# A three-part chain on one core: where the second MoE makes the next span's operand sums

## The chip, the cores and the metric

The kernel runs on one core of a Trainium2 chip. Its time is the device time in microseconds (us) of one execution; the median of three runs is compared. The engines of the core work side by side, each through its own list of instructions in order: TensorE (matmul), VectorE (called DVE in the rows), ScalarE (ACT), GpSimd (POOL) and SyncE (SP, which issues the DMAs here).

## What is computed

Decayed linear attention ("retention"), and two feed-forward stages on its 4608 tokens of width 512:

```python
x = retention(q, k, v)                          # 8 x 8 heads, 576 positions, width 64
h = max(x @ w1, x @ w2, x @ w3); x = h @ w_out  # first MoE, d_ff 768
h = x @ w_in                                    # second MoE: 512 -> 2048
g = h * clip(h + 3.0, 0.0, 6.0) / 6.0
out = g @ w_out                                 # 2048 -> 512
```

All of it is in float32 precision. The kernel gets that from split operands: a number is held as a high part (rounded by ScalarE to the type that TensorE takes) and a remainder (the difference, by VectorE), and a product is three matmuls: high x high, high x remainder, remainder x high.

## The kernel before

The change touches only how the second MoE makes the token operands of its first matmuls. That stage works on six *spans* of 768 tokens (index p), and in each span on eight *pairs* of hidden blocks (index j): a pair is 256 hidden units. In a pair the 512 x 768 tokens and the 512 x 256 weights are each cut in two by two, and the four hidden blocks C11, C22, C21 and C12 (128 x 384 each) come out of seven products instead of eight. Each product is six matmuls of 128x384. The products take, in this order, the token operands B11, B21, T2, T1, T3, T4, B22 (products 0 to 6), where the T's are sums of token quarters:

- T1 = B12 - B11, T2 = B22 - T1, T3 = B22 - B12, T4 = B21 - T2. Each is one subtraction on VectorE over 128x768 numbers (line 597), made in place in the span's tile `xf`: T1 takes B11's room, T3 takes B12's, T4 takes B21's.
- Each of the seven operands is then split (`split`, lines 53 to 56): ScalarE writes the high part (line 55, a CAST), and the remainder (line 56, VectorE) is put on a list, `late`. `flush()` empties that list into VectorE's order; it is called ahead of each projection job and ahead of each gate.

The function `operand(p, v, name)` does this for one operand. The operands of span p + 1 are made while span p is worked on: its tokens are loaded in pair 1, B11 and B21 are made in pair 4, T2 and T1 in pair 5, T3 and T4 in pair 7, and B22 in pair 0 of span p + 1 itself. B11, B21, T1 and T2 have a second set of tiles; T3, T4 and B22 have one, so their split may be written only when the last pair has read the old one (products 4, 5 and 6 of pair 7).

Two PSUM tiles, X and Y, hold the products of a pair, and the next pair uses the same two banks. What frees them is this. Product 0 goes to X, ScalarE copies it out (`kept`, line 674), products 2, 4 and 5 are added to X, with a copy after 2 and after 4; products 1, 3 and 6 go to Y. `added` (line 669, tile `cc`) adds Y and a copy, `gated` (lines 661 and 662, tile `g`) applies the activation and splits the result to tile `v`. C11 is gated after product 1, C22 after product 4, C21 after product 5 straight out of X, and C12 after product 6. So the next pair's product 0 waits for C21's line 662, and its product 1 for C12's line 669.

Between the products stand the projections: `project(2)` takes two jobs off a list of the pair before, each three matmuls of 128x512 (lines 703 to 705) that multiply a gated block by `w_out`. In pair 0 the last jobs of the span before are among them, and their results are brought out by ScalarE and VectorE in turn (`store`, lines 687 and 689).

The order of each engine's list is the order in which the code calls these functions (the schedule is manual); nothing reorders it later. The first span's operands are made in a loop beside the last tile of the first MoE, in the order `FRONT + BACK` (line 578).

Of the kernel before, what the change touches and what calls it, by code (L numbers as in the profile page):

```python
# [24 lines left out]
F1, F2 = FF1 // P, FF2 // P  # L25
# [4 lines left out]
NS = NT // TS  # L30
# [9 lines left out]
def retention_moe_moe2(ctx: ExitStack, tc, hi, lo, w_a, w_b, mask, qdec, kdec, grow, out):  # L40
# [3 lines left out]
    def f32(ap):  # L44
        return ap.bitcast(F32)
# [3 lines left out]
    def flush():  # L49
        while late:  # L50
            late.pop(0)()

    def split(full, hi, lo, eng=None):

        nc.scalar.copy(hi, full)  # L55
        late.append(lambda: (eng or nc.vector).tensor_tensor(out=lo, in0=full, in1=f32(hi), op=ALU.subtract))  # L56
# [16 lines left out]
    def x_tile():  # L73
        return x_pool.tile([P, 2, KM, TB], F32R, tag="x", name="x")
# [65 lines left out]
    def v_tile():  # L140
        return w_pool.tile([P, 2, 512], F32R, tag="v", bufs=NA - F2, name="v")
# [292 lines left out]
    def product(ps, w, cols, terms, first, last, read=False):  # L434

        xh, xl = terms
        wh, wl = w[:, 0, cols], w[:, 1, cols]
        nc.tensor.matmul(ps, lhsT=wh, rhs=xh, start=first, stop=False, skip_group_check=read)  # L438
        nc.tensor.matmul(ps, lhsT=wh, rhs=xl, start=False, stop=False, skip_group_check=read)  # L439
        nc.tensor.matmul(ps, lhsT=wl, rhs=xh, start=False, stop=last, skip_group_check=read)  # L440
# [45 lines left out]
    with tc.manual_schedule():  # L486
# [94 lines left out]
        def load_x2(p, room):  # L581

            full = room[:, :KM * TS].rearrange("p (k n) -> p k n", n=TS)
            n0 = 0
            while n0 < TS:
                t, c0 = divmod(p * TS + n0, TB)
                n = min(TB - c0, TS - n0)
                nc.sync.dma_start(out=full[:, :, n0:n0 + n], in_=x2_d[t][:, :, c0:c0 + n])
                n0 += n
            k2 = KM // 2  # L590
            return {"B11": full[:, :k2, :TH], "B12": full[:, :k2, TH:], "B21": full[:, k2:, :TH],
                    "B22": full[:, k2:, TH:], "X": room[:, KM * TS:].rearrange("p (k n) -> p k n", n=TH)}

        def operand(p, v, name):

            def put(out, a, b):
                nc.vector.tensor_tensor(out=out, in0=a, in1=b, op=ALU.subtract)
                return out

            if name == "T2":  # L600
                v["T1"] = put(v["B11"], v["B12"], v["B11"])
                v["T2"] = put(v["X"], v["B22"], v["T1"])
            elif name == "T3":
                v["T3"] = put(v["B12"], v["B22"], v["B12"])
            elif name == "T4":
                v["T4"] = put(v["B21"], v["B21"], v["T2"])
            pool = m2 if p % 2 and name in FRONT else xq_pool
            q = xq[p, name] = pool.tile([P, 2, KM // 2, TH], F32R, tag=name, name=name)
            split(v[name], q[:, 0], q[:, 1])

        for t in range(1, TT):
# [9 lines left out]
            for n, blk in enumerate(todo):  # L621
# [8 lines left out]
                if t == B:  # L630
                    if n == 1:
                        xv = load_x2(0, f32(x_tile()).rearrange("p a k n -> p (a k n)")[:, :KM * TS + TS])
# [20 lines left out]
        while names:  # L653
            operand(0, xv, names.pop(0))
# [3 lines left out]
        def gated(full, s0, f):  # L658

            g = m2.tile([P, TH], F32, tag="g", bufs=2, name="g")  # L660
            nc.vector.tensor_scalar(out=g, in0=full, scalar1=3.0, scalar2=0.0, op0=ALU.add, op1=ALU.max)
            nc.vector.scalar_tensor_tensor(out=g, in0=g, scalar=6.0, in1=full, op0=ALU.min, op1=ALU.mult)  # L662
            parts = v_tile()[:, :, :TH]
            split(g, parts[:, 0], parts[:, 1])
            return [(s0 + s, parts[:, :, s * P:(s + 1) * P], f) for s in range(TH // P)]

        def added(a, b):
            c = m2.tile([P, TH], F32, tag="cc", bufs=2, name="cc")
            nc.vector.tensor_tensor(out=c, in0=a, in1=b, op=ALU.add)  # L669
            return c  # L670

        def kept(ps):
            c = m2.tile([P, TH], F32, tag="c", bufs=4, name="c")
            nc.scalar.copy(c, ps)  # L674
            return c
# [8 lines left out]
        def store(p, s, ps):  # L684
            ob = f32(v_tile()).rearrange("p a n -> p (a n)")[:, :DM]
            if s % 2:
                nc.vector.tensor_scalar(out=ob, in0=ps, scalar1=1.0 / 6.0, scalar2=None, op0=ALU.mult)
            else:
                nc.scalar.mul(ob, ps, 1.0 / 6.0)
            t, s = divmod(p * TS // P + s, TB // P)  # L690
            for part, to in rows(t, s):
                nc.sync.dma_start(out=to, in_=ob[part])

        def project(n):

            for _ in range(min(n, len(todo))):
                flush()
                p, (s, g, f), start, stop = todo.pop(0)
                if start:
                    outs[s] = (ps_acc.tile([P, 512], F32, tag=f"o{s}", name=f"o{s}") if s < 4 else  # L700
                              ps_x.tile([P, 512], F32, tag=f"p{s}", name=f"p{s}"))
                gh, gl = g[:, 0], g[:, 1]
                nc.tensor.matmul(outs[s], lhsT=gh, rhs=wo[f][:, 0, :], start=start, stop=False)  # L703
                nc.tensor.matmul(outs[s], lhsT=gh, rhs=wo[f][:, 1, :], start=False, stop=False)  # L704
                nc.tensor.matmul(outs[s], lhsT=gl, rhs=wo[f][:, 0, :], start=False, stop=stop)  # L705
                if stop:
                    store(p, s, outs[s])
# [3 lines left out]
        for p, j in groups:  # L711
            after = groups[groups.index((p, j)) + 1:][:1]
            X, Y = (ps_mm.tile([P, 512], F32, tag="mm", name="mm")[:, :TH] for _ in range(2))
            new = {}

            def times(ps, q, name, first, last):
                w, x = wq[p, j][q], xq[p, name]
                for kk in range(KM // 2):
                    product(ps, w, slice(kk * P, (kk + 1) * P), (x[:, 0, kk, :], x[:, 1, kk, :]),
                            first and kk == 0, last and kk == KM // 2 - 1, read=True)  # L720
                if after and after[0] != (0, 1):
                    load_wq(*after[0], q)

            times(X, 0, "B11", True, True)
            if (p, j) == (0, 0):
                times(Y, 1, "B21", True, True)
                down(TT - 1, F1 - 1)
                flush()
                moe.release()
                x_pool.release()  # L730
                m2 = ctx.enter_context(tc.tile_pool(name="m2", bufs=1, reuse_waits="tile"))
                load_wq(0, 1)
            c1 = kept(X)
            project(2)
            if (p, j) != (0, 0):
                times(Y, 1, "B21", True, True)
            if j == 0 and p:
                operand(p, xv, "B22")
            elif j == 1 and p + 1 < NS:
                xv = load_x2(p + 1, m2.tile([P, KM * TS + TS], F32, tag="xf", name="xf"))  # L740
            elif 4 <= j < 6 and p + 1 < NS:
                operand(p + 1, xv, FRONT[2 * j - 8])
            flush()
            new["C11"] = gated(added(Y, c1), 0, 2 * j)
            project(2)
            times(X, 2, "T2", False, True)
            c2 = kept(X)
            project(2)
            times(Y, 3, "T1", True, True)
            if 4 <= j < 6 and p + 1 < NS:  # L750
                operand(p + 1, xv, FRONT[2 * j - 7])
            project(2)
            times(X, 4, "T3", False, True)
            c3 = kept(X)
            flush()
            new["C22"] = gated(added(Y, c3), TH // P, 2 * j + 1)
            project(2)
            times(X, 5, "T4", False, True)
            if j == F2 // 2 - 1 and p + 1 < NS:
                operand(p + 1, xv, "T3")  # L760
            flush()
            new["C21"] = gated(X, 0, 2 * j + 1)
            project(2)
            times(Y, 6, "B22", False, True)
            if j == F2 // 2 - 1 and p + 1 < NS:
                operand(p + 1, xv, "T4")
            flush()
            new["C12"] = gated(added(Y, c2), TH // P, 2 * j)
            for name in ("C11", "C22", "C21", "C12"):
                for job in new[name]:  # L770
                    todo.append((p, job, j == 0 and name in ("C11", "C22"),
                                 j == F2 // 2 - 1 and name in ("C21", "C12")))
# [56 lines left out]
```

## Time and profile before

| | us |
|---|---|
| median of three runs | 1555.58 |
| lowest and highest run | 1553.91 and 1557.76 |
| the profiled execution | 1551.59 |
| its span (first to last instruction) | 1549.8 |
| TensorE busy in it | 1484.6 |
| VectorE busy | 902.5 |
| ScalarE busy | 441.4 |

The second MoE fills the second half, from 757 us on. The timeline gives an instruction's start and length, and in brackets how long its engine stood before it and what ended that. TensorE's matmuls overlap: one of 128x384 is drawn with some 0.34 us, though the next starts about 0.17 after it, so a recorded gap is shorter than the time lost.

### The profile page before, as it was taken

How to read it: one execution, taken by the hardware profiler on the slowest of the kernel's cores; microseconds unless marked ns; L12 is line 12 of the kernel's file. 1: busy time of each engine (PE TensorE's matmuls, PEld its weight loads, DVE VectorE, ACT ScalarE, POOL GpSimd, SP SyncE). 2: the span in 40 equal slices, each digit the busy share in tenths (PEclk: the TensorE clock that was granted, in tenths of full speed). 3: DMA queues.
4: the chain of work that ended last, by engine and by line, in shares of the span. 5: the costliest groups of instructions: out<-in, count | busy, mean ns of one | idle time of the engine just before them, and what ended most of it. 6: DMA issues, size and time to landing. Idle time of an engine off the chain costs nothing.

```text
span 1549.8 us, 24664 instructions
## 1 busy us (share of the span) xinstructions
PE 1484.6 (96%) x9664; PEld 1258.9 (81%) x9664; DVE 902.5 (58%) x2019; ACT 441.4 (28%) x850; POOL 172.6 (11%) x196
## 2 busy tenths in 40 slices
PE   7689989999999999999999999989989999999998
PEld 4567878888888888888798889879878888888887
DVE  4886577767676757213446555555555555465453
ACT  3344224333333332112222222222222222222221
POOL 1445212312232222000000000000000000000000
PEclk9889999999999999999999999999999999999999
DMA  9563166656565553217454264445427436443431
GB/s 224 140 164 119 55 152 189 180 178 158 180 174 177 159 186 98 96 62 244 138 176 114 77 224 122 116 144 157 115 69 238 115 90 211 116 122 112 147 103 41
DMA packets 94660, 220.02 MB, mean 142 GB/s; under 512 B 18320, under 2 KB 21648, under 8 KB 90448
## 3 DMA queue, kind: packets, MB, share of 16 engines
q1 hardware_dynamic: 94544, 218.44, 47.7%
q8 instruction: 77, 1.26, 0.3%
q14 instruction: 39, 0.32, 0.1%
HBM read 174.36 MB, written 44.04 MB: 141 GB/s over the span
## 4 chain that ended last, share of the span: by engine, by line
PE 81%; DVE 11%; ACT 3%; DMA 3%; issue 1%; SPq 0%; ACTq 0%; POOL 0%; POOLq 0%; DVEq 0%
PE mm L438 16%; PE mm L440 15%; PE mm L439 15%; PE o L704 5%; PE o L705 5%; PE o L703 5%; PE o L438 3%; PE o L439 3%; PE o L440 3%; PE p L704 2%; PE p L703 2%; PE p L705 2%; PE at L310 2%; PE at L268 2%; DVE g L662 1%
## 5 line engine op out<-in xcount | busy, mean ns | idle before, releaser
L55 ACT CAST v<-g 128x384 fp32r<-128x384 f32 x192 | 98.5, 513 | 370.0 <-DVE g L662 361.3
L669 DVE TENSOR_TENSOR cc<-mm,c 128x384 f32<-128x384 f32 x144 | 79.9, 555 | 201.9 <-ACT c L674 191.7
L438 PE MATMUL mm<-x,w 128*128 128x512 f32 x468 | 190.1, 406 | 3.4 <-ACT t L453 3.0
L439 PE MATMUL mm<-x,w 128*128 128x512 f32 x468 | 184.9, 395 | 0.0
L440 PE MATMUL mm<-x,w 128*128 128x512 f32 x468 | 184.5, 394 | 0.0
L56 DVE TENSOR_TENSOR v<-g,v 128x384 fp32r<-128x384 f32 x192 | 107.2, 559 | 112.3 <-ACT v L55 112.3
L455 DVE TENSOR_TENSOR t<-mm,t 128x512 f32<-128x512 f32 x108 | 74.4, 689 | 136.6 <-PE mm L440 135.3
L704 PE MATMUL o<-w,v 128*128 128x512 f32 x384 | 152.3, 397 | 0.0
L705 PE MATMUL o<-w,v 128*128 128x512 f32 x384 | 152.0, 396 | 0.0
L703 PE MATMUL o<-w,v 128*128 128x512 f32 x384 | 151.7, 395 | 0.0
L438 PE MATMUL mm<-T,wq 128*128 128x384 f32 x384 | 130.6, 340 | 2.5 <-ACT c L674 1.8
L440 PE MATMUL mm<-T,wq 128*128 128x384 f32 x384 | 129.5, 337 | 0.0
L439 PE MATMUL mm<-T,wq 128*128 128x384 f32 x384 | 129.2, 337 | 0.0
L674 ACT COPY c<-mm 128x384 f32<-128x384 f32 x144 | 68.8, 478 | 178.7 <-PE mm L440 178.7
L438 PE MATMUL mm<-B,wq 128*128 128x384 f32 x288 | 99.5, 345 | 17.3 <-DVE g L662 13.0
L131 POOL TENSOR_TENSOR wf<-wf,wp 128x512 f32<-128x512 f32 x56 | 74.8, 1336 | 356.7 <-DVE wp L129 346.3
L438 PEld LDWEIGHTS mm<-x,w 128*128 128x128 f32 x468 | 89.4, 191 | 25.0 <-ACT t L453 4.0
L440 PEld LDWEIGHTS mm<-x,w 128*128 128x128 f32 x468 | 89.4, 191 | 19.3
L439 PEld LDWEIGHTS mm<-x,w 128*128 128x128 f32 x468 | 89.6, 192 | 17.3
L440 PE MATMUL mm<-B,wq 128*128 128x384 f32 x288 | 97.8, 339 | 0.0
L439 PE MATMUL mm<-B,wq 128*128 128x384 f32 x288 | 97.6, 339 | 0.0
L303 DVE SCALAR_TENSOR_TENSOR raw<-raw,at 64x64 f32<-64x64 f32 x392 | 85.9, 219 | 11.3
(129 smaller groups left out, 2903.3 us busy)
## 6 DMA issues: line engine op xcount, KB each, us to landing
wq<-wqd SPq DMA_DIRECT2D x336, 256.0 KB, 2.8
ws<-in_w_b SPq DMA_DIRECT2D x32, 512.0 KB, 7.2
raw<-in_hi SPq DMA_DIRECT2D x29, 560.0 KB, 5.6
raw<-in_lo SPq DMA_DIRECT2D x29, 560.0 KB, 7.7
ws<-in_w_a SPq DMA_DIRECT2D x24, 512.0 KB, 4.0
wqd<-y SPq DMA_DIRECT2D x24, 512.0 KB, 2.9
x2d<-y SPq DMA_DIRECT2D x18, 512.0 KB, 3.1
wod<-y SPq DMA_DIRECT2D x16, 512.0 KB, 3.0
```

The costliest lines, as they stand in the source:

```text
L55: nc.scalar.copy(hi, full)
L56: late.append(lambda: (eng or nc.vector).tensor_tensor(out=lo, in0=full, in1=f32(hi), op=ALU.subtract))
L131: nc.gpsimd.tensor_tensor(out=frac, in0=frac, in1=f32(power), op=ALU.mult)
L303: nc.vector.scalar_tensor_tensor(out=new, in0=old, scalar=gamma[2 * self.hp + e] ** C, in1=add, op0=ALU.mult, op1=ALU.add)
L438: nc.tensor.matmul(ps, lhsT=wh, rhs=xh, start=first, stop=False, skip_group_check=read)
L439: nc.tensor.matmul(ps, lhsT=wh, rhs=xl, start=False, stop=False, skip_group_check=read)
L440: nc.tensor.matmul(ps, lhsT=wl, rhs=xh, start=False, stop=last, skip_group_check=read)
L455: nc.vector.tensor_tensor(out=tmp[t, f], in0=ps, in1=tmp[t, f], op=ALU.max)
L669: nc.vector.tensor_tensor(out=c, in0=a, in1=b, op=ALU.add)
L703: nc.tensor.matmul(outs[s], lhsT=gh, rhs=wo[f][:, 0, :], start=start, stop=False)
L704: nc.tensor.matmul(outs[s], lhsT=gh, rhs=wo[f][:, 1, :], start=False, stop=False)
L705: nc.tensor.matmul(outs[s], lhsT=gl, rhs=wo[f][:, 0, :], start=False, stop=stop)
```

## The change

The sums for T3 and T4 are no longer made where these two are split. Both are made at T1's turn, in pair 5, right after T1's and T2's. Splitting T3, T4 and B22 moves as well: T3's behind C12's gate, at the end of pair 7 (before: ahead of C21's gate), and T4's together with B22's behind C11's gate in pair 0 of the next span (before: T4 ahead of C12's gate in pair 7, B22 ahead of C11's gate).

```diff
             if name == "T2":
                 v["T1"] = put(v["B11"], v["B12"], v["B11"])
                 v["T2"] = put(v["X"], v["B22"], v["T1"])
-            elif name == "T3":
+            elif name == "T1":
                 v["T3"] = put(v["B12"], v["B22"], v["B12"])
-            elif name == "T4":
                 v["T4"] = put(v["B21"], v["B21"], v["T2"])
...
-            if j == 0 and p:
-                operand(p, xv, "B22")
-            elif j == 1 and p + 1 < NS:
+            if j == 1 and p + 1 < NS:
                 xv = load_x2(p + 1, m2.tile([P, KM * TS + TS], F32, tag="xf", name="xf"))
             elif 4 <= j < 6 and p + 1 < NS:
                 operand(p + 1, xv, FRONT[2 * j - 8])
             flush()
             new["C11"] = gated(added(Y, c1), 0, 2 * j)
+            if j == 0 and p:
+                operand(p, xv, "T4")
+                operand(p, xv, "B22")
             project(2)
...
             times(X, 5, "T4", False, True)
-            if j == F2 // 2 - 1 and p + 1 < NS:
-                operand(p + 1, xv, "T3")
             flush()
             new["C21"] = gated(X, 0, 2 * j + 1)
             project(2)
             times(Y, 6, "B22", False, True)
-            if j == F2 // 2 - 1 and p + 1 < NS:
-                operand(p + 1, xv, "T4")
             flush()
             new["C12"] = gated(added(Y, c2), TH // P, 2 * j)
+            if j == F2 // 2 - 1 and p + 1 < NS:
+                operand(p + 1, xv, "T3")
```

TensorE's and SP's lists stay in the same order. What moves stands on VectorE and ScalarE. In the lists below line numbers behind 600 are smaller by one in the changed kernel (its code is two lines shorter), and the number behind a tile's name counts tiles.

VectorE in pair 5 of the first span, before: C11's gate and remainder (`v`), then T1's remainder, then C22's add.

```order
L669 TENSOR_TENSOR cc_7856<-mm_7825,c_7834 128x384
L661 TENSOR_SCALAR g_7858<-cc_7856 128x384
L662 SCALAR_TENSOR_TENSOR g_7858<-g_7858,cc_7856 128x384
L56 TENSOR_TENSOR v_7861<-g_7858,v_7861 128x384
L56 TENSOR_TENSOR T1_7894<-xf_7318,T1_7894 128x768
L669 TENSOR_TENSOR cc_7913<-mm_7825,c_7911 128x384
```

The same place now:

```order
L668 TENSOR_TENSOR cc_7856<-mm_7825,c_7834 128x384
L660 TENSOR_SCALAR g_7858<-cc_7856 128x384
L661 SCALAR_TENSOR_TENSOR g_7858<-g_7858,cc_7856 128x384
L56 TENSOR_TENSOR v_7861<-g_7858,v_7861 128x384
L597 TENSOR_TENSOR xf_7318<-xf_7318 128x2x384 x2
L56 TENSOR_TENSOR T1_7896<-xf_7318,T1_7896 128x768
L668 TENSOR_TENSOR cc_7915<-mm_7825,c_7913 128x384
```

The two sums of T3 and T4 (line 597, x2) have come in between C11's and T1's remainders.

VectorE at the change from the first span to the second, before: C22's remainder, then T3's sum and remainder ahead of C21's gate, T4's ahead of C12's add, and B22's remainder ahead of the next C11's add.

```order
L56 TENSOR_TENSOR v_8178<-g_8175,v_8178 128x384
L597 TENSOR_TENSOR xf_7318<-xf_7318 128x2x384
L56 TENSOR_TENSOR T3_8196<-xf_7318,T3_8196 128x768
L661 TENSOR_SCALAR g_8199<-mm_8092 128x384
L662 SCALAR_TENSOR_TENSOR g_8199<-g_8199,mm_8092 128x384
L56 TENSOR_TENSOR v_8202<-g_8199,v_8202 128x384
L597 TENSOR_TENSOR xf_7318<-xf_7318 128x2x384
L56 TENSOR_TENSOR T4_8220<-xf_7318,T4_8220 128x768
L669 TENSOR_TENSOR cc_8223<-mm_8093,c_8141 128x384
```

The same place now, one row further on:

```order
L56 TENSOR_TENSOR v_8180<-g_8177,v_8180 128x384
L660 TENSOR_SCALAR g_8197<-mm_8094 128x384
L661 SCALAR_TENSOR_TENSOR g_8197<-g_8197,mm_8094 128x384
L56 TENSOR_TENSOR v_8200<-g_8197,v_8200 128x384
L668 TENSOR_TENSOR cc_8217<-mm_8095,c_8143 128x384
L660 TENSOR_SCALAR g_8219<-cc_8217 128x384
L661 SCALAR_TENSOR_TENSOR g_8219<-g_8219,cc_8217 128x384
L56 TENSOR_TENSOR v_8222<-g_8219,v_8222 128x384
L56 TENSOR_TENSOR T3_8224<-xf_7318,T3_8224 128x768
L668 TENSOR_TENSOR cc_8254<-mm_8227,c_8236 128x384
```

C21's gate and C12's add follow C22's remainder directly; T3's remainder stands between C12's and the next C11's add.

ScalarE at the same change of span, before: T3's cast, C21's, T4's, C12's, the copy of the next pair's product 0, B22's, C11's, the next copy.

```order
L55 CAST T3_8196<-xf_7318 128x768
L55 CAST v_8202<-g_8199 128x384
L55 CAST T4_8220<-xf_7318 128x768
L55 CAST v_8228<-g_8225 128x384
L674 COPY c_8240<-mm_8230 128x384
L55 CAST B22_8257<-xf_7318 128x768
L55 CAST v_8265<-g_8262 128x384
L674 COPY c_8282<-mm_8230 128x384
```

The same place now:

```order
L55 CAST v_8200<-g_8197 128x384
L55 CAST v_8222<-g_8219 128x384
L55 CAST T3_8224<-xf_7318 128x768
L673 COPY c_8236<-mm_8226 128x384
L55 CAST v_8259<-g_8256 128x384
L55 CAST T4_8261<-xf_7318 128x768
L55 CAST B22_8263<-xf_7318 128x768
L673 COPY c_8282<-mm_8226 128x384
```

T3's cast now stands directly ahead of the copy after product 0, T4's and B22's directly ahead of the copy after product 2.

## Rows read from the trace of the kernel before

**Rows 1.** The page: shares of the chain that ended last, by engine

```profile
PE 81%; DVE 11%; ACT 3%; DMA 3%; issue 1%; SPq 0%; ACTq 0%; POOL 0%; POOLq 0%; DVEq 0%
```

**Rows 2.** TensorE's waits from 765 us on: us in total, times, longest

```profile
PE mm L438 <- DVE g L662: 13.0, 8, 2.2
PE mm L438 <- DVE cc L669: 4.2, 6, 1.7
```

**Rows 3.** Timeline, TensorE: start, length, line, tiles; marks behind product 0

```profile
835.20 0.39 PE L703 MATMUL o<-w,v 128*128 128x512 f32 x1
...
965.99 0.39 PE L703 MATMUL o<-w,v 128*128 128x512 f32 x1
...
982.13 0.39 PE L703 MATMUL o<-w,v 128*128 128x512 f32 x1
...
1442.02 0.39 PE L703 MATMUL o<-w,v 128*128 128x512 f32 x1
...
1489.05 0.39 PE L703 MATMUL o<-w,v 128*128 128x512 f32 x1
...
1520.42 0.39 PE L703 MATMUL o<-w,v 128*128 128x512 f32 x1
```

**Rows 4.** Timeline, TensorE, span 1 to 2: first matmuls of products 0 and 1

```profile
1014.84 0.44 PE L438 MATMUL mm<-B,wq 128*128 128x384 f32 x1 [2.24 <-DVE g L662]
...
1019.22 0.44 PE L438 MATMUL mm<-B,wq 128*128 128x384 f32 x1 [1.68 <-DVE cc L669]
```

**Rows 5.** Timeline, VectorE, pair 7 of span 1: from C22's add to C21's gate

```profile
1008.32 0.56 DVE L669 TENSOR_TENSOR cc<-mm,c 128x384 f32<-128x384 f32 x1 [5.13 <-ACT c L674]
...
1010.92 0.95 DVE L597 TENSOR_TENSOR xf<-xf 128x768 f32<-128x768 f32 x1
1012.77 0.96 DVE L56 TENSOR_TENSOR T<-xf,T 128x768 fp32r<-128x768 f32 x1 [0.90 <-ACT T L55]
...
1014.23 0.55 DVE L662 SCALAR_TENSOR_TENSOR g<-g,mm 128x384 f32<-128x384 f32 x1
```

**Rows 6.** Timeline, VectorE, pair 4 of span 1: C22's add and C21's gate

```profile
960.87 0.56 DVE L669 TENSOR_TENSOR cc<-mm,c 128x384 f32<-128x384 f32 x1 [2.63 <-ACT c L674]
...
964.05 0.55 DVE L662 SCALAR_TENSOR_TENSOR g<-g,mm 128x384 f32<-128x384 f32 x1
```

**Rows 7.** Timeline, ScalarE, pairs 4 and 5: C12's cast, the copy behind it

```profile
967.24 0.51 ACT L55 CAST v<-g 128x384 fp32r<-128x384 f32 x1 [2.08 <-DVE g L662]
967.65 0.47 ACT L674 COPY c<-mm 128x384 f32<-128x384 f32 x1
```

**Rows 8.** Timeline, VectorE, pair 5 of span 1: C11's remainder, C22's add, C21's gate

```profile
974.10 0.56 DVE L56 TENSOR_TENSOR v<-g,v 128x384 fp32r<-128x384 f32 x1 [0.58 <-ACT v L55]
...
976.95 0.56 DVE L669 TENSOR_TENSOR cc<-mm,c 128x384 f32<-128x384 f32 x1 [0.78 <-ACT c L674]
...
980.14 0.56 DVE L662 SCALAR_TENSOR_TENSOR g<-g,mm 128x384 f32<-128x384 f32 x1
```

**Rows 9.** Timeline, VectorE, last tile of the first MoE: a sum among others

```profile
743.63 0.69 DVE L455 TENSOR_TENSOR t<-mm,t 128x512 f32<-128x512 f32 x1 [2.03 <-PE mm L440]
744.24 0.95 DVE L597 TENSOR_TENSOR x<-x 128x768 f32<-128x768 f32 x1
745.11 0.69 DVE L56 TENSOR_TENSOR h<-t,h 128x512 fp32r<-128x512 f32 x1
```

**Rows 10.** Timeline, TensorE: first matmul of product 0, pair 6 of span 1

```profile
981.07 0.34 PE L438 MATMUL mm<-B,wq 128*128 128x384 f32 x1
```

**Rows 11.** Timeline, TensorE: first matmul of product 0, pair 1 of span 1

```profile
902.08 0.44 PE L438 MATMUL mm<-B,wq 128*128 128x384 f32 x1 [0.16 <-DVE g L662]
```

**Rows 12.** Windows, TensorE: length, busy (instructions), granted clock, DMA share, GB/s

```profile
884.03:888.42 4.39, 4.26 (x13) 0.61 0.00 0
1014.84:1019.22 4.38, 2.70 (x12) 1.00 0.00 0
...
1426.30:1534.70 108.40, 108.40 (x539) 1.00 0.37 111
```

## The prediction, made before the changed kernel was run

> **What bounds the kernel now.** I read the chain of work that ended last first: 81% of it is matmul and only 11% VectorE [rows 1]. The core waits for TensorE, so a change on VectorE pays only where TensorE stands still for it. The table of waits for the second MoE says where: TensorE waited 13.0 us for the second gate step (line 662) and 4.2 us for the add (line 669) [rows 2]. These recorded waits are too small, because the matmul before a gap is drawn with a modelled end and because some restarts after a gap are slow. So I measured the loss by marks: the first projection matmul behind product 0 of a pair. In the last span, which makes no operands for a next one, five pairs take 1520.42 - 1442.02 = 78.40, 15.68 us a pair. From pair 5 of the first span to pair 5 of the last, five spans of eight pairs take 1489.05 - 835.20 = 653.85, 130.77 a span; eight undisturbed pairs would take 125.44. Each change of span costs 5.33 us, 26.6 us in the kernel [rows 3].
>
> The timelines place it. At the change from span 1 to span 2 TensorE stands 2.24 us before product 0 (bank X still read by gate C21) and 1.68 us before product 1 (bank Y still read by the add of C12) [rows 4]. VectorE's row shows why: C22's add starts at 1008.32; then come T3's sum at 1010.92 and, after 0.90 us of standing for T3's cast on ScalarE, T3's remainder at 1012.77; only then C21's gate, ending 1014.23 + 0.55 = 1014.78, and product 0 starts 0.06 later [rows 4, 5]. T4's sum and remainder, which follow in the same way, do the same to C12's add and product 1.
>
> **The change, part by part.** No operation is added or removed: ten subtractions of 0.95 (T3, T4; five spans) and their casts and remainders change place. No DMA is among them, SP's list is the same in both orders, POOL has nothing in this stage.
>
> *T3 and T4 leave the places before C21 and C12.* Without them C21 follows C22's remainder as in any pair: there C22's add starts at 960.87 and C21's gate ends at 964.05 + 0.56 = 964.61, 3.74 later [rows 6]. From 1008.32 this gives 1012.06, plus 0.06. TensorE is done with product 6 at 1014.84 - 2.24 = 1012.60 [rows 4], so product 0 starts without a wait. C12's add follows as in any pair, and product 1 has none either. Next late would be C21 by some 0.4 us: the margin that every pair lives on.
>
> *T3 split behind C12.* T3's cast now stands on ScalarE between C12's cast and the copy of the next pair's X. In a plain pair these start at 967.24 and 967.65 [rows 7]; a cast of 128x768 takes 0.83 to 0.90 (the 0.90 of rows 5), so the copy moves from 967.65 to 968.5 and, lasting 0.47, ends at 969.0. Product 2, which adds into X, starts two projections after product 1; counted from the mark 965.99 [rows 3] that is 1.39 + 1.05 + 1.39 = 3.83 later, at 969.8 (six projection matmuls take 1.39 and a product of six 1.05, an estimate: seven products and six pairs of projections make 7.35 + 8.33 = 15.68). 0.8 us are left. T3's remainder runs from 968.5 and lets C11's add start at 969.4 instead of behind product 1 at 968.7 (0.96 less 0.08, below); Y is wanted again only by product 3 at 969.8 + 2.44 = 972.2, more than 2 us after that add. Cost zero; if the cover is gone, what exceeds 0.8 us, five times.
>
> *T4 and B22 split behind C11 of pair 0.* ScalarE gets two casts (1.7 to 1.8 us) before the copy of X after product 2; C11's cast ends 2.1 after its add (an estimate from C22 in rows 5: 1010.92 - 0.48 - 1008.32), at 971.5, the two casts at 973.2 to 973.3, the copy (0.47) by 973.8, and product 4, the next to need X, starts at 969.8 + 2 x 2.44 = 974.7. 0.9 us are left. VectorE's two remainders (0.96 each) end about 974.3, before C22's add, which waits for product 4 and its copy until about 976.5. Product 5 wants T4 at 974.7 + 2.4 = 977.1. Cost zero, with a margin to watch.
>
> *T3's and T4's sums behind T1 in pair 5.* This is the price. VectorE ran C11's remainder at 974.10 and reached C22's add at 976.95 after 0.78 us of waiting for the copy [rows 8]. Two sums now stand between that remainder and T1's. Independent operations overlap a little: a sum at 744.24 was followed by the next operation at 745.11, 0.87 later, though it lasts 0.95 [rows 9]. With this overlap of 0.08 everywhere, the chain from C11's remainder (0.56, the next 0.48 after it) is 974.10 + 0.48 + 3 x 0.87 = 977.19, C22's add 0.24 late (T1's remainder, which stood for its cast before, finds it done). With full lengths back to back it is 974.10 + 0.56 + 1.90 + 0.96 = 977.52, 0.57 late. C21's gate in that pair ended at 980.14 + 0.56 = 980.70 [rows 8], with the 0.06 at 980.76, and product 0 of pair 6 started at 981.07 [rows 10]: 0.31 of margin. So the stall is 0, or 0.26 and 0.1 more for the restart: 0 to 0.4 us a span. I take 0, by the rows that overlap; 0.4 is kept for the range, 2 us in all.
>
> The page "VectorE: DVE Perf Modes" of the Trainium skill, in "The DRAIN you can't avoid", says that an operation does not start before the pipeline of the one ahead is empty. By that the stall would be the 0.4 and the sum 2 us dearer; the row at 745.11 starts before its predecessor ended and speaks against it.
>
> *The first span.* Its operands are made beside the last tile of the first MoE; two sums move ahead of an h remainder. VectorE stood 2.03 us there before the maximum [rows 9], more than 1.9, and h is wanted several blocks later. Cost zero; at worst 1.9 us once.
>
> **Sum.** Of 5.33 us a span two losses stay: pair 5's own, from T2's two sums, 982.13 - 965.99 = 16.14, 0.46 over [rows 3]; and the wait before product 0 of pair 1, 0.16 recorded at 902.08 [rows 11], from the output's evictions among the gates, about 0.4 with the lost overlap and the slow restart (0.44 for 0.34). 5.33 - 0.46 - 0.40 = 4.47, five times 22.3 us. The profiled run lasted 1551.59 (span 1549.80): 1529.3, span 1527.5. It was 4.0 faster than the median of the runs, 1555.58; off that median I forecast **1533.3 us**.
>
> **The rivals.**
>
> 1. *Pair 5 pays in full.* T1's cast ends up behind the sums instead of beside them: 974.66 + 1.90, cast 0.9, remainder 0.96, C22 at 978.4, 1.5 late, less the margin of 0.31, plus 0.1: 1.3 x 5 = 6.4, **1540**. For it: T2, whose cast does follow its sums, costs 0.46 in this same pair. Against: T1's data are ready earlier and its cast waits for no sum. 8%.
>
> 2. *T3's cast, or those of T4 and B22, holds the copy that product 2 or 4 needs.* The margins are 0.8 and 0.9; a queue 1 to 2 us later than counted costs 0.2 to 1.2 a span, 1 to 6 us: **1534 to 1540**, 1537 in the middle. For it: three casts in a row on an engine served in order. 6%.
>
> 3. *The clock gives more.* After the gap before product 0 the granted clock was 0.61 over 4.39 us in one change of span (half rate, 1.2 GHz, for most of it) and 1.00 in another [rows 12]; three of the five look like the first. If each gave back 4.39 x 0.39 = 1.7, 5 us more: **1528**. Against: product 1 started 4.38 to 4.39 after product 0 in both, since VectorE set it; the slow clock cost nothing. 3%. The page "TensorE: Matmul & The Clock Gate" of the Trainium skill ("Terms") puts the penalty of a throttled stretch at its length times the share of pulses lost; by that this would be the sum, and the trace disagrees.
>
> 4. *It doesn't do what it says.* VectorE's chain alone, without T3 and T4, holds X and Y at the change of span, so that under 4.7 us come back: **1551 to 1556**. Against: plain pairs run the same chain at 15.68. 4%.
>
> 5. *Slower.* TensorE without rests gets less clock. Place: the whole stage, 772 us. From a granted clock 3% lower on, the 22 us are eaten; at 4% it costs 31, **1564**. Against: the last span ran 108.4 us without a rest at 1.00 [rows 12]. 3%.
>
> **How the numbers follow.** The forecast, 1531 to 1537, has 76%. Range 1529 to 1540: forecast, rivals 1 and 2, pair 5's 0.4, the 1.9 of the first span, and the 2 us that runs of the kernel before lie from their median. What a measurement of this kernel can tell from no change is about 0.3%, 4.7 us. Faster: forecast and rivals 1 to 3, 93%, rounded down to 0.92 for what I have not listed; same 0.04; slower 0.04.
>
> **What would show it.** Right: the mark-to-mark time of a span falls from 130.8 to about 126.3, the waits for lines 661 and 668 (as they are then) in this stage shrink to under 3 us, product 0 and product 1 follow without a gap at the change of span, C22's add in pair 5 starts 0.2 to 0.6 later without a gap before product 0 of pair 6. Wrong: a new gap before product 0 of pair 6 (rival 1), before product 2 or 4 of pair 0 with a ScalarE copy as releaser (rival 2), marks in plain pairs longer than 15.68 (rival 5).

## The result

The changed kernel takes 1530.16 us (median of four runs, 1527.50 to 1532.58) against 1554.74 for the kernel before: ratio 0.985, 95% interval 0.983 to 0.987. Beside later kernels on another occasion it took 1529.72 (five runs) against 1552.54, ratio 0.985 (0.983 to 0.987). It is 23 to 25 us faster; 22.3 was forecast, and 1530.16 lies in the range, 3 us below the forecast time.

The page of the changed kernel: its span, then the shares of the chain that ended last, which answer to [rows 1].

```profile
span 1530.8 us, 24657 instructions
...
PE 85%; DVE 9%; DMA 3%; ACT 2%; issue 1%; SPq 0%; POOL 0%; ACTq 0%; POOLq 0%; DVEq 0%
```

The table of TensorE's waits in the second MoE (us in total, times, longest) answers to [rows 2]. The 13.0 and 4.2 us have become 1.9 and 0.4, and 1.4 of the 1.9 belong to the first pair of all, as does the whole row of ScalarE's copies (ACT); these stood in the kernel before too.

```profile
PE mm L438 <- DVE g L661: 1.9, 4, 1.4
PE mm L438 <- ACT c L673: 1.8, 3, 1.1
PE mm L438 <- DVE cc L668: 0.4, 2, 0.2
```

The marks (first projection matmul behind product 0), in TensorE's timeline, answer to [rows 3]: pair 5 of the first span, pairs 5 and 6 of span 1, pairs 0 and 1 of span 2, pair 5 of the last.

```profile
838.44 0.39 PE L702 MATMUL o<-w,v 128*128 128x512 f32 x1
...
964.81 0.39 PE L702 MATMUL o<-w,v 128*128 128x512 f32 x1
...
980.94 0.39 PE L702 MATMUL o<-w,v 128*128 128x512 f32 x1
...
1012.29 0.39 PE L702 MATMUL o<-w,v 128*128 128x512 f32 x1
...
1028.35 0.40 PE L702 MATMUL o<-w,v 128*128 128x512 f32 x1
...
1470.02 0.39 PE L702 MATMUL o<-w,v 128*128 128x512 f32 x1
```

From the first to the last of them five spans take 1470.02 - 838.44 = 631.58, 126.32 a span; it was 130.77, and 126.3 was forecast. So five changes of span give 22.3 us back, to a tenth what the sum said. What is left of the loss is also where the sum left it: pair 5 takes 980.94 - 964.81 = 16.13, 0.45 over, and pair 0 takes 1028.35 - 1012.29 = 16.06, 0.38 over.

The change of span itself, VectorE's timeline (start, length, line, tiles, idle time before), answers to [rows 5]:

```profile
1007.13 0.56 DVE L668 TENSOR_TENSOR cc<-mm,c 128x384 f32<-128x384 f32 x1 [5.13 <-ACT c L673]
...
1010.31 0.56 DVE L661 SCALAR_TENSOR_TENSOR g<-g,mm 128x384 f32<-128x384 f32 x1
...
1011.93 0.55 DVE L668 TENSOR_TENSOR cc<-mm,c 128x384 f32<-128x384 f32 x1
...
1014.78 0.96 DVE L56 TENSOR_TENSOR T<-xf,T 128x768 fp32r<-128x768 f32 x1 [0.18 <-ACT T L55]
```

C21's gate now ends 1010.31 + 0.56 - 1007.13 = 3.74 after C22's add starts, as in a plain pair [rows 6], where it was 6.46 [rows 5]. TensorE starts product 0 at 1011.25, 0.38 after that gate, and product 1 at 1013.68, both without a gap (their rows answer to [rows 4]):

```profile
1011.25 0.34 PE L438 MATMUL mm<-B,wq 128*128 128x384 f32 x1
...
1013.68 0.34 PE L438 MATMUL mm<-B,wq 128*128 128x384 f32 x1
```

**Where the other 2 us are.** The medians lie 24.6 apart and the marks give 22.3; the two profiled spans lie only 1549.8 - 1530.8 = 19.0 apart. The difference is in front of the stage. The first matmul that follows the copy of the first pair started at these times in the kernel before, in the changed kernel, and in a second profile of the same changed kernel (each row from TensorE's timeline of its own trace):

```profile
763.11 0.44 PE L438 MATMUL mm<-T,wq 128*128 128x384 f32 x1 [1.06 <-ACT c L674]
```
```profile
766.34 0.44 PE L438 MATMUL mm<-T,wq 128*128 128x384 f32 x1 [1.06 <-ACT c L673]
```
```profile
763.46 0.45 PE L438 MATMUL mm<-T,wq 128*128 128x384 f32 x1 [1.06 <-ACT c L673]
```

One kernel, twice: 2.9 us apart. Between the first two of these rows lie 766.34 - 763.11 = 3.23 us, and 19.0 + 3.2 gives the marks' 22.3 to a tenth: for the two profiled executions the front accounts for the difference. Over the ten profiles of this study, whose first 700 us hold the same work in the same order, this row lies between 761.1 and 766.3. So the front adds some us of chance to every execution, and the marks inside the stage are the better measure: the two profiles of the changed kernel both give 126.32 us a span.

### The profile page after: what moved, and what is told of

It is laid out like the page before. It is cut to its first block, busy times and chain, and to the rows that moved or that the text cites. A ratio compares the mean times of both kernels' runs of the same rounds, so it can differ in the third digit from the quotient of the medians.

```text
span 1530.8 us, 24657 instructions
## 1 busy us (share of the span) xinstructions
PE 1480.5 (97%) x9664; PEld 1258.2 (82%) x9664; DVE 902.1 (59%) x2019; ACT 440.0 (29%) x850; POOL 172.4 (11%) x196
## 4 chain that ended last, share of the span: by engine, by line
PE 85%; DVE 9%; DMA 3%; ACT 2%; issue 1%; SPq 0%; POOL 0%; ACTq 0%; POOLq 0%; DVEq 0%
PE mm L438 17%; PE mm L439 16%; PE mm L440 16%; PE o L703 5%; PE o L704 5%; PE o L702 5%; PE o L438 3%; PE o L439 3%; PE o L440 3%; PE p L703 2%; PE p L702 2%; PE p L704 2%; PE at L310 2%; PE at L268 2%; DMA raw<-in_lo 2%; DVE g L661 1%
## 5 line engine op out<-in xcount | busy, mean ns | idle before, releaser
L439 PEld LDWEIGHTS mm<-x,w 128*128 128x128 f32 x468 | 89.3, 191 | 17.2
L438 PE MATMUL mm<-B,wq 128*128 128x384 f32 x288 | 97.8, 340 | 2.1 <-DVE g L661 1.9
L440 PE MATMUL mm<-B,wq 128*128 128x384 f32 x288 | 97.0, 337 | 0.0
L439 PE MATMUL mm<-B,wq 128*128 128x384 f32 x288 | 96.9, 336 | 0.0
```

## The experiments

Two theories. *A*, the prediction's: VectorE's list is served in order, so what stands ahead of the gate that frees X (C21) and of the add that frees Y (C12) is paid in full beyond the margin that the release has: the sum, the standing for the cast, the remainder; what stands behind them is free. *B*: the work is the price; the gain comes from the 1.9 us of sums taken out of the crowded change of span and done early, and the places of the splits matter little. The change does both at once, so the first two runs take it apart.

### The sums early, the splits in their old places

The kernel before, with this alone:

```diff
-            elif name == "T3":
+            elif name == "T1":
                 v["T3"] = put(v["B12"], v["B22"], v["B12"])
-            elif name == "T4":
                 v["T4"] = put(v["B21"], v["B21"], v["T2"])
```

> Half of the change: T3's and T4's sums at T1's turn in pair 5 as in the changed kernel, but the three splits in their old places (T3 ahead of C21's gate, T4 ahead of C12's, B22 ahead of C11's). Theory A (VectorE's list in order: all that stands ahead of C21 and C12 counts, the sum, the standing for the cast and the remainder): T3's cast can start at once behind C22's, so C21 is delayed by 1.1 us instead of 2.7; X comes free 4.9 us after C22's add starts, TensorE is there at 4.1: 0.8 to 0.9 us before product 0, 0.2 to 0.3 before product 1. Mark to mark 127.5 us a span (before 130.77, changed 126.32), 16 us less than before: ratio to before 0.989 to 0.991. Theory B (the work is the price: 1.9 us of sums taken out of the change of span, the places of the splits matter little): the whole gain, 126.3 a span, ratio 0.985 to 0.986.

Measured: 1535.90 against 1553.73 (ratio 0.989, 0.987 to 0.990); marks 836.22 and 1473.86, 127.53 a span. The marks, then VectorE's timeline at the same change of span, and the matmul that waited:

```profile
836.22 0.39 PE L702 MATMUL o<-w,v 128*128 128x512 f32 x1
...
1473.86 0.39 PE L702 MATMUL o<-w,v 128*128 128x512 f32 x1
```
```profile
1006.07 0.56 DVE L668 TENSOR_TENSOR cc<-mm,c 128x384 f32<-128x384 f32 x1 [5.13 <-ACT c L673]
...
1008.93 0.96 DVE L56 TENSOR_TENSOR T<-xf,T 128x768 fp32r<-128x768 f32 x1 [0.18 <-ACT T L55]
...
1010.39 0.56 DVE L661 SCALAR_TENSOR_TENSOR g<-g,mm 128x384 f32<-128x384 f32 x1
```
```profile
1011.00 0.44 PE L438 MATMUL mm<-B,wq 128*128 128x384 f32 x1 [0.65 <-DVE g L661]
```

T3's remainder alone still stands ahead of C21's gate and holds it to 4.88 after the add. The standing for the cast has shrunk from 0.90 to 0.18, since the cast no longer waits for a sum. So the early sums alone bring 130.77 - 127.53 = 3.24 of the 4.45, which is not B's whole gain, and the time a span follows A to 0.03 us. TensorE's one recorded gap there is 0.65 us, but by the marks pair 7 takes 16.6 (plain 15.7) and pair 0 of the next span 0.3 more than in the changed kernel, so product 1 is late as well, as expected.

### The splits moved, the sums where they are split

The changed kernel with the sums' branches of the kernel before: the diff above, turned round.

> The other half: T3 split behind C12's gate, T4 and B22 behind C11's gate of pair 0, but each sum made right at its split as before, none in pair 5. Theory A: C21 and C12 have nothing ahead of them, so no wait before product 0 or 1. The sums now stand before their casts: the copy after product 0 ends at about 969.4 on the scale of pair 5 of the kernel before, product 2 wants it at 969.8, the copy after product 2 comes 0.9 later than in the changed kernel, with 1.4 us to spare there. Mark to mark 126.3 to 126.5 a span, pair 5 still at 16.1 (T2's sums): ratio to before 0.985 to 0.986. Theory B: the sums still fall in the change of span, so most of the loss stays, 129 or more a span, ratio above 0.994.

Measured: 1528.46 against 1553.73 (0.984, 0.982 to 0.986); marks 834.69 and 1466.39, 126.34 a span. The whole gain, with no sum made early. The marks, then VectorE behind C12's gate:

```profile
834.69 0.39 PE L703 MATMUL o<-w,v 128*128 128x512 f32 x1
...
1466.39 0.39 PE L703 MATMUL o<-w,v 128*128 128x512 f32 x1
```
```profile
1009.15 0.56 DVE L662 SCALAR_TENSOR_TENSOR g<-g,cc 128x384 f32<-128x384 f32 x1
1009.62 0.95 DVE L597 TENSOR_TENSOR xf<-xf 128x768 f32<-128x768 f32 x1
1010.49 0.55 DVE L56 TENSOR_TENSOR v<-g,v 128x384 fp32r<-128x384 f32 x1
1011.48 0.96 DVE L56 TENSOR_TENSOR T<-xf,T 128x768 fp32r<-128x768 f32 x1 [0.43 <-ACT T L55]
```

T3's sum, the standing and the remainder are all there, in the crowded place, and cost nothing, because the gate that frees X and the add that frees Y are ahead of them. B is out: it wanted 129 or more. Of the two halves of the change either helps, but the second suffices, and the first adds nothing to it that the marks show (126.32 with, 126.34 without).

### T3 alone

The kernel before, with T3's sum at T1's turn and its split behind C12's gate; T4 and B22 stay.

```diff
-            elif name == "T3":
+            elif name == "T1":
                 v["T3"] = put(v["B12"], v["B22"], v["B12"])
...
-            if j == F2 // 2 - 1 and p + 1 < NS:
-                operand(p + 1, xv, "T3")
             flush()
             new["C21"] = gated(X, 0, 2 * j + 1)
...
             new["C12"] = gated(added(Y, c2), TH // P, 2 * j)
+            if j == F2 // 2 - 1 and p + 1 < NS:
+                operand(p + 1, xv, "T3")
```

> T3 alone as in the changed kernel (sum at T1's turn, split behind C12); T4 and B22 in their old places with T4's sum there. Theory A: no gap before product 0, but T4's sum, the standing for its cast and its remainder hold C12's add by 2.7 us against some 0.9 of margin: a gap of 1.6 to 1.8 before product 1, mark to mark 128.0 to 128.2. Theory B (half of the work moved, half of the gain): a gap before both, 128.5.

Measured: one run of 1538.63; marks 834.81 and 1476.07, 128.25 a span. TensorE's only recorded gap at the change to span 2, and VectorE's rows that make it:

```profile
1013.58 0.44 PE L438 MATMUL mm<-B,wq 128*128 128x384 f32 x1 [1.47 <-DVE cc L669]
```
```profile
1010.19 0.95 DVE L597 TENSOR_TENSOR xf<-xf 128x768 f32<-128x768 f32 x1
1012.10 0.96 DVE L56 TENSOR_TENSOR T<-xf,T 128x768 fp32r<-128x768 f32 x1 [0.95 <-ACT T L55]
1012.97 0.55 DVE L669 TENSOR_TENSOR cc<-mm,c 128x384 f32<-128x384 f32 x1
```

Product 0 is free, product 1 pays for T4, 0.05 above what A said. The two gaps have one cause each.

### A third sum in pair 5

The changed kernel with one more subtraction beside the two that pair 5 took on. Nothing reads what it writes.

```diff
                 v["T4"] = put(v["B21"], v["B21"], v["T2"])
+                if p:
+                    put(v["X"], v["B22"], v["T4"])
```

> The changed kernel with one more subtraction of 128x768 on VectorE beside T3's and T4's sums in pair 5, into a room that nothing reads any more (in the spans after the first). It doubles half of the price that the prediction put at nothing. Theory A (0.31 us of margin before product 0 of pair 6, of which the two sums used 0.16, so that 0.09 are left behind the 0.06): 0.87 us more on VectorE is 0.8 of stall and 0.1 of restart, pair 5 at 17.0 instead of 16.12, mark to mark 127.2, 4.5 us in all, ratio to before 0.987 to 0.989. Rival (the pair's idle time on VectorE takes a third sum as it took two): 126.3, the changed kernel's time.

Measured: 1535.62 against 1553.73 (0.989, 0.987 to 0.990); marks 837.41 and 1473.89, 127.30 a span. VectorE and TensorE:

```profile
973.29 2.81 DVE L597 TENSOR_TENSOR xf<-xf 128x768 f32<-128x768 f32 x3
976.02 0.95 DVE L56 TENSOR_TENSOR T<-xf,T 128x768 fp32r<-128x768 f32 x1
...
980.07 0.56 DVE L663 SCALAR_TENSOR_TENSOR g<-g,mm 128x384 f32<-128x384 f32 x1
```
```profile
980.68 0.44 PE L438 MATMUL mm<-B,wq 128*128 128x384 f32 x1 [0.72 <-DVE g L663]
```

One sum more and product 0 of pair 6 waits: 127.30 - 126.32 = 0.98 us a span. The sum itself takes 0.99 us of VectorE, not the expected 0.87: T1's remainder starts 976.02 - 973.29 = 2.73 after the first sum, with two sums 1.74, since the third reads what the second wrote and does not start until that is done. Less the 0.09 of margin and with the 0.1 of restart that is the 1.0 measured. The place that the changed kernel used for two sums had room for two and no third. The same two sums are as free where they are split (second experiment above) and, in the next two runs, in pair 6.

### T2 behind C11 as well

If A holds, the loss that stays in pair 5 has the same cure: T2's two sums and its split stand ahead of C11's add, which frees Y for product 3. Here they go behind C11's gate, and T3's and T4's sums go to pair 6.

```diff
-            elif 4 <= j < 6 and p + 1 < NS:
-                operand(p + 1, xv, FRONT[2 * j - 8])
+            elif j == 4 and p + 1 < NS:
+                operand(p + 1, xv, "B11")
             flush()
             new["C11"] = gated(added(Y, c1), 0, 2 * j)
+            if j == 5 and p + 1 < NS:
+                operand(p + 1, xv, "T2")
+            if j == 6 and p + 1 < NS:
+                back_sums(xv)
```

(`back_sums` makes T3's and T4's sums; T1's turn makes them in the first span only.)

> The changed kernel with the same step done to T2: in pair 5 its sums and split stand behind C11's gate instead of ahead of C11's add, and T3's and T4's sums stand in pair 6, behind C11's gate. Theory A (what stands ahead of a gate or add in VectorE's list is paid, what stands behind it is free): the 0.44 that pair 5 loses before product 3 goes, and nothing new comes, since the copy after product 2 is held to 973.4 on the scale of the first trace and product 4 wants it at 974.7. Pair 5 at 15.68, mark to mark 125.9. Rival (T2's cast, which now waits for two sums, holds that copy too long, or VectorE is too full between C11 and C22): pair 5 stays at 16.1 or more, 126.3.

Measured: one run of 1530.31, in an execution whose front was late (the row of 763.11 stood at 766.08); marks 838.18 and 1467.74, 125.91 a span. The loss of pair 5 is gone and no other came.

### And one eviction less on VectorE

The run before, and `store` gives the fourth of the six evictions to ScalarE:

```diff
-            if s % 2:
+            if s in (1, 5):
                 nc.vector.tensor_scalar(out=ob, in0=ps, scalar1=1.0 / 6.0, scalar2=None, op0=ALU.mult)
```

> As the run before, and of the six evictions of the output in pair 0 the fourth goes to ScalarE, so that VectorE has none between C22's and C21's gate. Theory A: the 0.4 before product 0 of pair 1 goes too, pair 0 at 15.7, mark to mark 125.5, that is the 125.44 of undisturbed pairs: TensorE without a loss at the change of span. 4 us less than the changed kernel, ratio to before 0.981 to 0.983. Rival (the eviction holds C21's cast or the next copy on ScalarE): pair 0 stays at 16.0 to 16.1, 125.9.

Measured: 1524.45 against 1552.54 (0.981, 0.979 to 0.983), and 5.3 us below the changed kernel's 1529.72 on the same chip. Marks 834.50 and 1461.92, 125.48 a span. TensorE in this kernel, from mark to mark (windows: length, busy time, granted clock, DMA share, GB/s):

```profile
834.50:1461.92 627.42, 627.42 (x3121) 1.00 0.47 140
```

Five spans without a recorded gap on TensorE, at the full clock. This version beats both the kernel before and the changed kernel.

### The same without early sums

The kernel just shown, with T3's and T4's sums made at their splits, as in the second experiment.

> As the run before, but T3's and T4's sums are made right at their splits, as in the run with the splits moved alone, and none early. If the place of the sums is free where the splits stand behind C12 and C11, as theory A has it, mark to mark is the same 125.5 and the ratio to before 0.981 to 0.983. If the early sums carry part of the gain (theory B), 127 or more.

Measured: 1524.34 against 1552.54 (0.982, 0.979 to 0.984), marks 833.19 and 1460.76, 125.51 a span. The place of the sums makes no difference here either, so the simplest winning edit moves four calls of `operand` (T2, T3, T4, B22), with the sums that belong to them, and changes one condition in `store`.

### The changed kernel again

> The changed kernel as it is, beside the two runs before on the same chip: ratio to before 0.985, 126.3 mark to mark; the first 765 us, which the change leaves alone but for the first span's sums, differ from run to run by some 3 us.

Measured: 1529.72 (0.985, 0.983 to 0.987), marks 835.55 and 1467.17, 126.32 a span, as the first time.

## Why the prediction was right

*What bounds the kernel.* Right. The loss was read from marks, 5.33 us a span, and not from the recorded waits (17.2 us, with those of the first pair); the marks came out to 0.02 us.

*T3 and T4 leave.* Right: C21's gate at 3.74 behind C22's add, as the row of a plain pair said (3.73 there; the prediction added 0.56 for the 0.55 of [rows 6]). The prediction did not say which half of the change does it. The runs do: the place behind the gate does it alone; early sums alone bring 3.24 of 4.45.

*The splits behind C12 and C11 cost nothing.* Right, with margins somewhat larger than counted. ScalarE's rows of the changed kernel from C12's cast on:

```profile
1013.50 0.51 ACT L55 CAST v<-g 128x384 fp32r<-128x384 f32 x1 [2.08 <-DVE g L661]
1013.92 0.83 ACT L55 CAST T<-xf 128x768 fp32r<-128x768 f32 x1
1014.65 0.47 ACT L673 COPY c<-mm 128x384 f32<-128x384 f32 x1
1017.23 0.51 ACT L55 CAST v<-g 128x384 fp32r<-128x384 f32 x1 [2.11 <-DVE g L661]
1017.65 0.83 ACT L55 CAST T<-xf 128x768 fp32r<-128x768 f32 x1
1018.39 0.83 ACT L55 CAST B<-xf 128x768 fp32r<-128x768 f32 x1
1019.12 0.47 ACT L673 COPY c<-mm 128x384 f32<-128x384 f32 x1
```

The copy after product 0 ends at 1015.12 and product 2 started at 1016.11: 1.0 to spare, 0.8 counted. The copy after product 2 ends at 1019.59 and product 4 started at 1020.98: 1.4, 0.9 counted. The count took a cast of 128x768 as 0.83 to 0.90 apiece; in a row they follow each other after 0.73, because in these rows ScalarE's operations overlap as VectorE's do (each starts some 0.1 before the one ahead ends). The starts of products 2 and 4 on TensorE:

```profile
1016.11 0.34 PE L438 MATMUL mm<-T,wq 128*128 128x384 f32 x1
...
1020.98 0.34 PE L438 MATMUL mm<-T,wq 128*128 128x384 f32 x1
```

*Pair 5's price.* Right, and by the value chosen. VectorE's rows in pair 5 of span 1, which answer to [rows 8]:

```profile
972.93 0.56 DVE L56 TENSOR_TENSOR v<-g,v 128x384 fp32r<-128x384 f32 x1 [0.58 <-ACT v L55]
973.40 1.82 DVE L597 TENSOR_TENSOR xf<-xf 128x768 f32<-128x768 f32 x2
975.14 0.95 DVE L56 TENSOR_TENSOR T<-xf,T 128x768 fp32r<-128x768 f32 x1
976.01 0.55 DVE L668 TENSOR_TENSOR cc<-mm,c 128x384 f32<-128x384 f32 x1
...
979.19 0.56 DVE L661 SCALAR_TENSOR_TENSOR g<-g,mm 128x384 f32<-128x384 f32 x1
```

Product 0 of pair 6, on TensorE, answers to [rows 10]:

```profile
979.90 0.34 PE L438 MATMUL mm<-B,wq 128*128 128x384 f32 x1
```

C22's add comes 976.01 - 964.81 = 11.20 after the mark, before 976.95 - 965.99 = 10.96: 0.24 late, the forecast figure. The two sums and T1's remainder start 0.87 apart (973.40, then 975.14 for two), so the rows decide against the full lengths, by which the add would have been 0.57 late. The sentence of the Trainium skill's page "VectorE: DVE Perf Modes" ("The DRAIN you can't avoid") that stands in the prediction doesn't hold for these rows; the same section adds that an operation that is not held starts earlier, and this is what they show. C21's gate ends at 979.75 and product 0 started at 979.90: of the margin some 0.1 is left behind the 0.06 of a release, and the run with a third sum used it up and paid the rest. Rival 1 is out: T1's cast did not stand behind the sums, and its remainder follows them without idle time.

*The two losses that stay.* Right in size (0.46 and 0.40 in the sum, 0.45 and 0.38 by the marks) and in cause: with T2 behind C11's gate pair 5 of span 1 takes 15.70, and with one eviction less on VectorE pair 0 of the spans takes 15.67.

*The first span.* Right, cost zero: from 700 us to the copy of the first pair TensorE has no recorded wait in either kernel, and the matmul behind that copy stands 1.06 us for it in both.

*The rivals.* 2 is out by ScalarE's rows above. 3 is out by the sum: 22.3 us without a term for the clock, which was 1.00 in the changed kernel's window over a change of span:

```profile
871.00:902.00 31.00, 30.84 (x154) 1.00 0.27 83
```

The slow stretch of [rows 12] lay inside a wait for VectorE and was worth nothing: in the kernel before, the granted clock in this stretch was 0.61 to 0.63 at three changes of span and 1.00 at two, and the five spans took 130.74 to 130.79 us all the same. 4 is out by the marks. 5 is out: plain pairs still take 15.64 to 15.73, and the kernel without any gap held 1.00 over 627 us.

*What was off* is 3.1 us between the forecast time, 1533.3, and the median, 1530.16. Of it 0.8 is the kernel before, which measured 1554.74 beside the changed one where the forecast started from 1555.58. The stage gives the 22.3 us, and the other 2.3 are no more than the front of the kernel varies by. That it is the front in those very runs is argued, not shown, since only one of them has a trace.

## What to carry to other kernels

On an engine that works its list in order, sort by what an instruction releases: first what frees a buffer that the bounding engine waits for, then the work whose result is wanted late. A preparation that sits ahead of such a release costs its own time and every wait of its own on a third engine, as far as they exceed the margin that the release has (here 0.31 us before product 0 of pair 6, which is why two sums ahead of C22's add in pair 5 were free and a third was not); behind the release the same work, in the same crowded stretch, can cost nothing, and here moving it to a quieter stretch gained no more. Measure such losses with marks in the bounding engine's timeline, since recorded gaps leave out part of them (here 17.2 us recorded, with the first pair's, against 26.6 by the marks).

## What the runs showed that was not expected

The front of the kernel, the same work every time but for the place of the first span's sums, took from 761.1 to 766.3 us in ten profiles, more than the difference between some of the kernels compared here. Between the first two of these profiles the 3.2 us had built up by 240 us in VectorE's timeline and stayed constant from there on; what causes them was not tried. And two subtractions that depend on each other take 1.94 to 1.95 us together, two that don't 1.82, and three of which the third reads what the second wrote 2.81: about 0.1 us of each operation is hidden under the next if it needn't wait for its result.
